# Two frequency pairs per filtered sum and half copy, under a newly written order of all instructions

## The chip, the cores and the metric

One core of one Trainium2 chip runs the whole kernel. The core's engines are TensorE (PE; its weight loads, PEld, overlap its matmuls), VectorE (DVE), ScalarE (ACT), GpSimd (POOL) and SyncE (SP), which here only issues DMAs. Each runs its own list of instructions in order and waits on semaphores for the others. The metric is the device time of one execution in microseconds (us). The kernel before takes 202.03 us (median of 3 runs, 201.94 to 202.16).

## The reference, cut to what matters

```python
x = A_x                                   # 1 x 2048 x 640, bf16
xn = layernorm(x)                         # over the 640 columns
X = rfft2(xn); X = X * (w_r + 1j * w_i)   # 2048 x 321 complex filter
A = irfft2(X, s=(2048, 640)).astype(bf16)
B = ((xn @ w_gate) * (xn @ w_up)) @ w_down   # 640 -> 1536 -> 640
return x + A + B
```

## The kernel before

The kernel computes the gated product (GLU) and the filtered spectrum in one program, so that TensorE always has matmuls of the one to run while the other engines prepare the other.

**Stages.** (1) Layer norm of 16 blocks of 128 rows (`bn`/`sm`/`sq`, `sd`, `rs`, `mul`), and transposes of the result. (2) GLU: each task `GU` is five matmuls of 512 columns (L951; the first blocks are smaller, L971), `eG` copies its PSUM bank to SBUF, and `H` multiplies gate and up (L987). (3) Column transform: `S1` to `S5` on DVE fold the 640 columns, `R` multiplies (L911), `eR` evicts. (4) The spectrum stage, described below. (5) Inverse over the columns: `I` (L1145), `eI`, `V1` to `V5` on DVE, `IV` (L1234). (6) `ACC` accumulates the GLU's second product (L1222) in a PSUM bank in three chunks (5, 4 and 3 matmuls, the last number of its name being 0, 5 or 9), `IV` adds the inverse transform into the same bank, `FINA` evicts it, `FIN` adds x, and a DMA stores it.

**The spectrum stage** runs over 16 steps t, each with two frequency pairs q = 2t and 2t+1:

- `D_t_0`, `D_t_1` (five matmuls each, L1028), evicted by `eD` (two copies of 64x321 each);
- `C_t` (two matmuls of 321 columns, L1048), which needs both `eD` of the step;
- `WM_t` on DVE: four products of 128x256 with the filter (L1065) into buffer PR, and two of 128x130 (L1071) into buffer Y5;
- `SM_t` on DVE: real and imaginary part of the filtered spectrum from PR, a subtraction on partitions 0 to 63 (L1080) and an addition on 64 to 127 (L1081), each 64x512, into buffer L;
- `JA_t` and `JB_t`: copies of the two halves of L across the partitions, the second negated, each 64x512, each on ACT or on DVE as the order says;
- `NS_t` on POOL: three copies inside Y5;
- `IA_2t`, `IA_2t+1` (four matmuls on L, L1114, two on Y5, L1116), evicted by `eIA` (128x320) into Z2. All 16 `I` need the whole of Z2, so all 32 `eIA`.

PR has two buffers of one step, L and Y5 three (`yr = t % 3`), the SBUF copy of D three.

**What sets the order.** `_PLAN` is one list of triples: task number, engine (0 PE, 1 ACT, 2 DVE, 3 POOL, 4 SP) and first PSUM bank (or -1). `replay` turns it into each engine's own list and derives the waits from reads, writes and bank owners. Nothing is decided at run time: an engine whose next instruction waits stands still, whatever lies behind it. PSUM has 8 banks; a matmul task that takes a bank waits for the evictions of the bank's last owner.

Of the kernel before, what the change touches and what calls it, by code (L numbers as in the profile page):

```python
# [369 lines left out]
_NY = 3  # L370
# [29 lines left out]
def _d_act(n):  # L400
# [4 lines left out]
    (12, 4, -1), (0, 1, -1), (13, 4, -1), (176, 1, -1), (175, 4, -1), (8, 2, -1), (18, 2, -1), (19, 2, -1), (20, 2, -1),  # L405
    (9, 3, -1), (29, 2, -1), (21, 1, -1), (23, 2, -1), (22, 2, -1), (11, 0, 0), (24, 2, -1), (25, 0, 2), (28, 2, -1),
    (30, 2, -1), (33, 2, -1), (177, 4, -1), (10, 0, 4), (178, 4, -1), (27, 2, -1), (14, 4, -1), (15, 4, -1), (31, 1, -1),
    (26, 1, -1), (185, 0, 5), (32, 2, -1), (34, 2, -1), (35, 0, 6), (179, 4, -1), (187, 0, 4), (36, 1, -1), (37, 2, -1),
    (180, 4, -1), (181, 4, -1), (38, 2, -1), (186, 1, -1), (39, 2, -1), (188, 1, -1), (189, 2, -1), (40, 2, -1), (192, 0, 0),
    (48, 2, -1), (41, 1, -1), (182, 4, -1), (197, 0, 1), (190, 0, 2), (198, 1, -1), (43, 2, -1), (195, 0, 3), (193, 1, -1),  # L410
    (16, 4, -1), (202, 0, 6), (42, 2, -1), (183, 4, -1), (196, 1, -1), (184, 4, -1), (44, 2, -1), (47, 2, -1), (1, 4, -1),
    (49, 2, -1), (191, 1, -1), (45, 0, 7), (200, 0, 5), (194, 2, -1), (17, 4, -1), (52, 2, -1), (50, 1, -1), (51, 2, -1),
    (2, 4, -1), (46, 1, -1), (53, 2, -1), (199, 2, -1), (205, 0, 4), (118, 2, -1), (201, 1, -1), (203, 1, -1), (54, 0, 5),
    (204, 2, -1), (207, 0, 1), (55, 1, -1), (3, 4, -1), (206, 1, -1), (210, 0, 0), (208, 1, -1), (119, 2, -1), (209, 2, -1),
    (211, 1, -1), (217, 0, 3), (120, 2, -1), (68, 1, -1), (215, 0, 2), (59, 2, -1), (69, 1, -1), (212, 0, 7), (57, 2, -1),
    (56, 2, -1), (60, 2, -1), (58, 2, -1), (4, 4, -1), (121, 2, -1), (218, 1, -1), (61, 2, -1), (220, 0, 6), (222, 0, 3),
    (213, 1, -1), (216, 1, -1), (214, 2, -1), (5, 4, -1), (62, 1, -1), (6, 4, -1), (122, 2, -1), (63, 2, -1), (70, 1, -1),
    (225, 0, 7), (219, 2, -1), (125, 0, 4), (71, 1, -1), (221, 1, -1), (7, 4, -1), (226, 1, -1), (230, 0, 2), (72, 1, -1),
    (64, 2, -1), (227, 0, 1), (66, 2, -1), (127, 2, -1), (123, 0, 6), (223, 1, -1), (73, 2, -1), (224, 2, -1), (128, 2, -1),
    (65, 4, -1), (78, 1, -1), (67, 4, -1), (231, 1, -1), (232, 0, 0), (76, 2, -1), (237, 0, 3), (129, 2, -1), (79, 1, -1),  # L420
    (228, 1, -1), (74, 2, -1), (80, 1, -1), (233, 1, -1), (235, 0, 2), (229, 2, -1), (81, 1, -1), (82, 1, -1), (236, 1, -1),
    (130, 2, -1), (75, 4, -1), (234, 2, -1), (83, 2, -1), (238, 1, -1), (240, 0, 1), (88, 1, -1), (242, 0, 0), (241, 1, -1),
    (131, 2, -1), (77, 4, -1), (84, 2, -1), (243, 1, -1), (85, 4, -1), (89, 1, -1), (126, 1, -1), (245, 0, 2), (247, 0, 3),
    (124, 1, -1), (134, 0, 0), (90, 1, -1), (246, 1, -1), (239, 2, -1), (86, 2, -1), (91, 1, -1), (92, 1, -1), (136, 2, -1),
    (244, 2, -1), (137, 2, -1), (87, 4, -1), (248, 1, -1), (252, 0, 4), (250, 0, 5), (93, 2, -1), (437, 4, -1), (132, 0, 6),
    (257, 0, 2), (249, 2, -1), (255, 0, 3), (438, 4, -1), (439, 4, -1), (251, 1, -1), (98, 1, -1), (138, 2, -1), (253, 1, -1),
    (260, 0, 5), (258, 1, -1), (254, 2, -1), (262, 0, 4), (139, 2, -1), (99, 1, -1), (256, 1, -1), (100, 1, -1), (440, 4, -1),
    (261, 1, -1), (441, 4, -1), (101, 1, -1), (263, 1, -1), (259, 2, -1), (267, 0, 2), (265, 0, 3), (272, 0, 5), (102, 1, -1),
    (96, 2, -1), (442, 4, -1), (266, 1, -1), (140, 2, -1), (270, 0, 4), (103, 2, -1), (443, 4, -1), (444, 4, -1), (268, 1, -1),
    (133, 1, -1), (264, 2, -1), (141, 0, 2), (94, 2, -1), (275, 0, 6), (104, 2, -1), (445, 4, -1), (108, 1, -1), (277, 0, 7),  # L430
    (142, 1, -1), (269, 2, -1), (446, 4, -1), (271, 1, -1), (145, 0, 2), (106, 2, -1), (273, 1, -1), (135, 1, -1), (280, 0, 4),
    (149, 2, -1), (276, 1, -1), (147, 0, 0), (278, 1, -1), (274, 2, -1), (150, 2, -1), (281, 1, -1), (447, 4, -1), (282, 0, 5),
    (279, 2, -1), (109, 1, -1), (146, 1, -1), (143, 0, 6), (285, 0, 4), (110, 1, -1), (448, 4, -1), (111, 1, -1), (477, 4, -1),
    (290, 0, 2), (287, 0, 3), (283, 1, -1), (151, 2, -1), (286, 1, -1), (291, 1, -1), (478, 4, -1), (288, 1, -1), (284, 2, -1),
    (152, 2, -1), (292, 0, 5), (112, 1, -1), (297, 0, 4), (479, 4, -1), (289, 2, -1), (148, 1, -1), (113, 2, -1), (153, 2, -1),
    (300, 0, 2), (293, 1, -1), (116, 2, -1), (144, 1, -1), (95, 4, -1), (97, 4, -1), (298, 1, -1), (114, 2, -1), (302, 0, 3),
    (294, 2, -1), (295, 0, 0), (307, 0, 1), (160, 0, 6), (156, 0, 4), (162, 2, -1), (105, 4, -1), (107, 4, -1), (301, 1, -1),
    (480, 4, -1), (296, 1, -1), (299, 2, -1), (303, 1, -1), (163, 2, -1), (158, 0, 2), (161, 1, -1), (305, 0, 0), (308, 1, -1),
    (154, 0, 6), (312, 0, 1), (481, 4, -1), (304, 2, -1), (159, 1, -1), (310, 0, 2), (482, 4, -1), (483, 4, -1), (317, 0, 3),
    (484, 4, -1), (306, 1, -1), (315, 0, 0), (155, 1, -1), (164, 2, -1), (318, 1, -1), (311, 1, -1), (115, 4, -1), (313, 1, -1),  # L440
    (157, 1, -1), (316, 1, -1), (309, 2, -1), (165, 2, -1), (322, 0, 6), (117, 4, -1), (320, 0, 7), (166, 2, -1), (319, 2, -1),
    (167, 0, 2), (323, 1, -1), (321, 1, -1), (314, 2, -1), (169, 0, 4), (168, 1, -1), (435, 4, -1), (170, 2, -1), (171, 0, 0),
    (173, 0, 6), (436, 4, -1), (172, 2, -1), (729, 4, -1), (513, 4, -1), (514, 4, -1), (324, 2, -1), (174, 1, -1), (325, 0, 2),
    (449, 0, 3), (515, 4, -1), (450, 2, -1), (326, 1, -1), (451, 0, 4), (465, 0, 5), (463, 0, 6), (452, 1, -1), (327, 0, 7),
    (453, 0, 0), (487, 0, 4), (485, 0, 2), (516, 4, -1), (464, 1, -1), (466, 2, -1), (454, 2, -1), (330, 0, 3), (501, 0, 5),
    (458, 3, -1), (335, 0, 6), (517, 4, -1), (328, 1, -1), (329, 2, -1), (467, 0, 0), (455, 2, -1), (486, 1, -1), (518, 4, -1),
    (468, 2, -1), (488, 1, -1), (519, 4, -1), (523, 0, 7), (331, 1, -1), (502, 1, -1), (337, 0, 2), (336, 1, -1), (332, 0, 3),
    (521, 0, 6), (499, 0, 4), (489, 0, 0), (456, 2, -1), (469, 2, -1), (340, 0, 5), (338, 1, -1), (520, 4, -1), (524, 1, -1),
    (342, 0, 2), (549, 4, -1), (457, 2, -1), (535, 0, 7), (333, 1, -1), (472, 3, -1), (461, 0, 3), (334, 2, -1), (522, 1, -1),
    (500, 1, -1), (459, 0, 6), (471, 1, -1), (490, 2, -1), (343, 1, -1), (550, 4, -1), (339, 2, -1), (345, 0, 4), (460, 1, -1),  # L450
    (503, 0, 0), (470, 1, -1), (352, 0, 2), (557, 0, 6), (491, 2, -1), (341, 1, -1), (551, 4, -1), (462, 1, -1), (504, 2, -1),
    (552, 4, -1), (536, 1, -1), (473, 0, 5), (347, 0, 3), (344, 2, -1), (559, 0, 7), (537, 0, 0), (475, 0, 1), (553, 4, -1),
    (505, 2, -1), (474, 1, -1), (353, 1, -1), (492, 2, -1), (508, 3, -1), (346, 1, -1), (506, 2, -1), (350, 0, 2), (494, 3, -1),
    (525, 0, 4), (476, 1, -1), (554, 4, -1), (555, 4, -1), (556, 4, -1), (348, 1, -1), (493, 2, -1), (349, 2, -1), (507, 2, -1),
    (355, 0, 1), (526, 2, -1), (360, 0, 3), (558, 1, -1), (495, 0, 6), (351, 1, -1), (354, 2, -1), (511, 0, 2), (538, 1, -1),
    (356, 1, -1), (497, 0, 0), (571, 0, 1), (361, 1, -1), (539, 0, 4), (585, 4, -1), (496, 1, -1), (586, 4, -1), (527, 2, -1),
    (587, 4, -1), (540, 2, -1), (357, 0, 3), (498, 1, -1), (362, 0, 6), (572, 1, -1), (595, 0, 0), (509, 0, 1), (358, 1, -1),
    (560, 1, -1), (365, 0, 3), (588, 4, -1), (596, 1, -1), (529, 2, -1), (573, 0, 7), (589, 4, -1), (512, 1, -1), (359, 2, -1),
# [67 lines left out]
def _build(nc, A_x, A_w_r, A_w_i, B_w_gate, B_w_up, B_w_down, out, opts=None):  # L526
# [3 lines left out]
    with es:  # L530
# [32 lines left out]
        b_g = alloc("G", 640)  # L563
        b_sm = alloc("SM", 384)
        b_gbf = alloc("GBF", 6 * 512)
        b_stat = alloc("STAT", 768)
        b_dum = alloc("DUM", 256)
        b_jk = alloc("JK", 640)

# [776 lines left out]
```

## Time and profile before

| | |
|---|---|
| median of 3 runs | 202.03 us |
| profiled execution: own time, span | 201.94 us, 200.1 us |
| busy: PE, DVE, ACT, POOL | 194.3, 179.1, 141.7, 24.8 us |
| granted TensorE clock | 1.000 |
| SM: 32 instructions of 64x512 on DVE | 422 and 420 ns each |
| JA on DVE, JA on ACT (64x512) | 12 of 298 ns, 4 of 628 ns |
| JB on DVE, JB on ACT (64x512) | 9 of 289 ns, 7 of 628 ns |

The profile's busy times say how long an engine had at least one instruction in flight; neighbouring instructions on one engine overlap a little, so an engine that never waits follows its own list at a spacing somewhat under the duration of an instruction. Matmul ends are modelled, so the spacing from one start to the next says more on PE than the busy time. The span runs from the first to the last instruction; 1.8 us of the execution lie around it.

### The profile page before, as it was taken

To read this page: it belongs to the slowest core of one execution; us is meant where nothing else is said; L and a number is where in the kernel's file an instruction comes from. 1 tells how busy PE (TensorE), PEld (TensorE's weight loads), DVE (VectorE), ACT (ScalarE), POOL (GpSimd) and SP (SyncE) were. 2 spreads that over 40 slices of the span, in tenths; PEclk is the share of its full clock that TensorE was granted. 3 is DMA by queue.
4 is the path that set the end of the run, shared out by engine and by line. 5 is a ranking of instruction groups with operands and counts; after the bars stand their busy time and mean duration, and the time that the engine had idled before them with its cause. 6 is when DMAs were issued, how large, how long until landed. Compare 5 with 4: busy or idle time off the path is not lost.

```text
span 200.1 us, 4335 instructions
## 1 busy us (share of the span) xinstructions
PE 194.3 (97%) x1623; PEld 123.3 (62%) x1623; DVE 179.1 (89%) x418; ACT 141.7 (71%) x309; POOL 24.8 (12%) x53
## 2 busy tenths in 40 slices
PE   7799999999999999999999999999999999999995
PEld 7698644445455555555555554547777777777774
DVE  3799999999999999989999989978999999899803
ACT  3377999999965989999999999996504541442311
POOL 0000000000000006056335333630000000000000
DMA  6999985428438351351452420006101325033422
GB/s 182 307 332 385 375 132 123 114 58 98 103 65 268 110 133 38 97 128 38 113 150 54 118 64 6 0 3 183 50 0 63 86 84 164 33 101 112 142 80 66
DMA packets 29669, 23.80 MB, mean 119 GB/s; under 512 B 10576, under 2 KB 27600, under 8 KB 29520
## 3 DMA queue, kind: packets, MB, share of 16 engines
q1 hardware_dynamic: 28848, 23.16, 42.1%
q10 hardware_dynamic: 800, 0.36, 0.7%
q8 instruction: 13, 0.21, 0.5%
q14 instruction: 8, 0.07, 0.1%
HBM read 18.92 MB, written 2.62 MB: 108 GB/s over the span
## 4 chain that ended last, share of the span: by engine, by line
PE 53%; ACT 26%; DVE 15%; issue 4%; DMA 1%
PE ps L1222 26%; ACT arena L687 20%; PE ps L951 12%; PE ps L971 6%; DVE arena L987 2%; PE ps L1145 2%; PE ps L1234 2%; ACT arena L750 2%; ACT arena L741 2%; ACT arena L1091 2%; DVE arena L863 1%; PE ps L1028 1%; DMA arena<-in_A_x_dram 1%; DVE arena L864 1%; PE ps L1048 1%
## 5 line engine op out<-in xcount | busy, mean ns | idle before, releaser
L687 ACT ACTIVATE arena<-ps 128x512 bf16<-128x512 f32 (+7 forms) x247 | 118.2, 529 | 47.2 <-PE ps L1234 21.1
L951 PE MATMUL ps<-arena 128*128 128x512 bf16 x420 | 98.1, 379 | 0.7 <-ACT arena L687 0.4
L951 PEld LDWEIGHTS ps<-arena 128*128 128x128 bf16 x420 | 38.4, 98 | 42.6 <-ACT arena L687 3.2
L1222 PE MATMUL ps<-arena 128*128 128x320 bf16 (+2 forms) x396 | 57.3, 295 | 0.0
L1222 PEld LDWEIGHTS ps<-arena 128*128 128x128 bf16 x396 | 37.6, 98 | 13.2
L1065 DVE TENSOR_TENSOR arena<-ps,arena 128x256 bf16<-128x256 f32 x64 | 22.7, 416 | 0.8 <-PE ps L1048 0.4
L1100 POOL COPY arena<-arena 128x126 bf16<-128x126 bf16 x16 | 6.6, 414 | 108.7 <-DVE arena L1071 108.7
L987 DVE TENSOR_TENSOR arena<-arena 128x512 bf16<-128x512 bf16 x42 | 17.4, 417 | 1.7 <-ACT arena L687 1.3
L971 PE MATMUL ps<-arena 128*128 128x128 bf16 (+1 forms) x160 | 14.1, 246 | 0.8 <-DVE arena L785 0.8
L971 PEld LDWEIGHTS ps<-arena 128*128 128x128 bf16 x160 | 12.3, 98 | 1.9 <-DMA arena<-in_B_w_gate_dram 0.8
L1261 DVE TENSOR_TENSOR arena<-arena 128x640 bf16<-128x640 bf16 x15 | 7.2, 486 | 6.1 <-ACT arena L687 6.1
L1102 POOL TENSOR_SCALAR arena<-arena 128x130 bf16<-128x130 bf16 x16 | 11.4, 715 | 0.0
L1028 PEld LDWEIGHTS ps<-arena 128*128 128x128 bf16 x160 | 7.5, 98 | 4.1 <-issue 0.4
L1114 PEld LDWEIGHTS ps<-arena 128*128 128x128 bf16 x128 | 7.6, 120 | 3.7 <-ACT arena L687 1.5
L1114 PE MATMUL ps<-arena 128*128 128x64 bf16 x128 | 8.9, 200 | 0.4 <-ACT arena L687 0.3
L688 DVE CAST arena<-ps 64x321 bf16<-64x321 f32 (+3 forms) x14 | 7.7, 577 | 1.6 <-PE ps L1116 1.1
L1028 PE MATMUL ps<-arena 128*128 128x64 bf16 (+1 forms) x160 | 8.5, 193 | 0.0
L750 ACT ACTIVATE arena<-arena 128x640 bf16<-128x640 bf16 x10 | 8.4, 839 | 0.1
L1071 DVE TENSOR_TENSOR arena<-ps,arena 128x130 bf16<-128x130 f32 x32 | 8.0, 293 | 0.0
L759 DVE BATCH_NORM_STATS2 arena<-arena 128x6 f32<-128x320 bf16 x12 | 5.3, 477 | 2.9 <-DMA arena<-in_A_x_dram 2.8
L863 DVE TENSOR_TENSOR arena<-arena 128x768 f32<-128x768 bf16 (+1 forms) x10 | 7.9, 789 | 0.0
L1101 POOL COPY arena<-arena 128x126 bf16<-128x126 bf16 x16 | 7.8, 490 | 0.0
(66 smaller groups left out, 211.9 us busy)
## 6 DMA issues: line engine op xcount, KB each, us to landing
arena<-in_A_x_dram SPq DMA_DIRECT2D x20, 160.0 KB, 2.6
arena<-in_A_w_r_dram SPq DMA_DIRECT2D x30, 80.2 KB, 2.2
arena<-in_A_w_i_dram SPq DMA_DIRECT2D x30, 80.2 KB, 2.2
out_dram<-arena SPq DMA_DIRECT2D x15, 160.0 KB, 1.8
arena<-in_B_w_gate_dram SPq DMA_DIRECT2D x4, 320.0 KB, 5.4
arena<-in_A_x_dram SPq DMA_DIRECT2D x1, 1280.0 KB, 10.0
arena<-c_tf SPq DMA_DIRECT2D x4, 256.0 KB, 10.2
arena<-c_ti SPq DMA_DIRECT2D x2, 512.0 KB, 5.3
```

Source lines behind the costliest of these rows:

```text
L687: return c.e.activation(dst, src, _ACTF.Copy)
L750: return c.e.activation(v_jk, v_x[:, b, :], _ACTF.Square, scale=-1.0, bias=v_m32[:, b:b + 1], accum_out=v_ss[:, b:b + 1])
L863: c.e.tensor_tensor(uo[:, o, :, 0:3, :], v_xb[:, b:b + nt, 0:6:2, :], v_xb[:, b:b + nt, 5:10:2, :], op)
L951: ins = c.e.matmul(ps[:, bk, :], v_gw[:, w, j, ft, :], v_xt[:, j, rows], start=(j == 0), stop=(j == 4))
L971: ins = c.e.matmul(ps[:, bk, w * n:(w + 1) * n], v_gw[:, w, j, ft, :], v_xt[:, j, rows], start=(j == 0), stop=(j == 4))
L987: return c.e.tensor_tensor(v_ht[:, ft0, rows], v_gbf[:, rr, 0, :], v_gbf[:, rr, 1, :], _OP.mult)
L1028: ins = c.e.matmul(ps[:, bk, k * 64:k * 64 + n], v_uq[:, k, t, :], v_fd[:, k * 128 + w * n: k * 128 + w * n + n], start=True, stop=True)
L1065: c.e.tensor_tensor(dst, xh, wv, _OP.mult)
L1071: ins = c.e.tensor_tensor(d5[w], ps[:, bk:bk + 2, 256:321], wt[:, w, :, 0:321:5], _OP.mult)
L1102: return c.e.tensor_scalar(yg[:, :, 128:193], yg[:, :, 256:321], -1.0, None, _OP.mult)
L1114: c.e.matmul(ps[:, bk, 64 * k:64 * k + 64], yl[:, k:512:4], v_ti[:, q, 0, :], start=True, stop=True)
L1222: ins = c.e.matmul(ps[:, bk, 0:sl3.stop - sl3.start], v_ht[:, ft, a * 128:(a + 1) * 128], v_wd[:, ft, sl3], start=(ft == _FT_ORDER[0]), st ...
```

## The change

1. `SM`, `JA` and `JB` run once for two steps: the loop leaves at even t after `NS_t`; at odd t one `SM_t` takes both steps' products (64x1024 per instruction), one `JA_t` and one `JB_t` copy 64x1024, and the four `IA` (and `eIA`) of the two steps follow. 48 tasks (64 instructions) become 24 (32 instructions).
2. Buffers: PR becomes one buffer of two steps, L two buffers of two steps (4096 elements instead of 3072). Y5 keeps three buffers of one step. STAT is 160 elements shorter, so what is allocated behind it moves by that much.
3. `_PLAN` is new throughout: order on every engine, engine of each eviction and half copy, PSUM banks. The list of SP is the same, entry by entry; POOL's differs in the order of a few `NS`.

```diff
-        b_pr = alloc("PR", 2 * 1024)
-        b_l = alloc("L", _NY * 1024)
+        b_pr = alloc("PR", 2048)
+        b_l = alloc("L", 2 * 2048)
...
-                        dst = v_pr[:, pb, w].rearrange("p g (h m k) -> p h g m k", h=2, k=4)[:, h]
+                        dst = v_pr[:, w, 2 * pb:2 * pb + 2].rearrange("p g (h m k) -> p h g m k", h=2, k=4)[:, h]
...
-            def em_sm(c, pb=pb, yr=yr):
-                pa_, pb_ = v_pr[:, pb, 0], v_pr[:, pb, 1]
-                c.e.tensor_tensor(v_l[0:64, yr, :, 0, :], pa_[0:64], pb_[64:128], _OP.subtract)
-                return c.e.tensor_tensor(v_l[64:128, yr, :, 0, :], pa_[64:128], pb_[0:64], _OP.add)
-            T("SM_%d" % t, "dve", 886.0, em_sm, reads=[(b_pr, ("r", pb, pb + 1))],
-              writes=[(b_l, ("r", 3 * yr, 3 * yr + 1))], prio=pq - 0.001)
...
+            if t % 2 == 0:
+                continue
+            lr = (t // 2) % 2
+
+            def em_sm(c, lr=lr):
+                pa_, pb_ = v_pr[:, 0], v_pr[:, 1]
+                c.e.tensor_tensor(v_l[0:64, lr, :, 0, :], pa_[0:64], pb_[64:128], _OP.subtract)
+                return c.e.tensor_tensor(v_l[64:128, lr, :, 0, :], pa_[64:128], pb_[0:64], _OP.add)
+            T("SM_%d" % t, "dve", 1420.0, em_sm, reads=[(b_pr, ("r", 0, 2))],
+              writes=[(b_l, ("r", 3 * lr, 3 * lr + 1))], prio=pq - 0.001)
...
+            for q in range(2 * t - 2, 2 * t + 2):
+                g, tq = q % 2, q // 2
+                yr = tq % _NY
```

The engine lists that the two plans give, counted by task:

| | ACT before | ACT after | DVE before | DVE after |
|---|---|---|---|---|
| SM | | | 16 | 8 (double) |
| JA | 4 | 3 (double) | 12 | 5 (double) |
| JB | 7 | 0 | 9 | 8 (double) |
| eD (two copies each) | 29 | 30 | 3 | 2 |
| eG | 97 | 95 | 3 | 5 |
| eR | 14 | 15 | 2 | 1 |
| eIA | 29 | 27 | 3 | 5 |
| eI | 15 | 14 | 1 | 2 |

All other counts are equal. Three stretches of the new lists, by name, that the prediction follows:

```
PE  (into the spectrum stage): 56 GU tasks in all, then R_15 R_12 R_13 GU_2_8_0 R_14 GU_2_8_1 D_0_1 D_1_0 D_0_0 D_1_1
    (before:                   56 GU tasks in all, then R_12 R_13 R_14 R_15 GU_2_8_0 D_0_0 D_0_1 D_1_1 D_1_0)
PE  (end of it): C_14 GU_9_12_0 IA_24 IA_25 C_15 GU_11_12_1 GU_11_12_0 IA_27 ACC_1_1_0 IA_26 GU_10_12_0 ACC_0_0_0
    IA_28 IA_30 IA_31 IA_29 ACC_0_0_5 I_1 I_0 I_2 ACC_1_1_5 I_3 I_6 ACC_0_1_0 ACC_2_0_0 I_4 ACC_0_1_5 ACC_2_0_5 ACC_0_1_9 I_7
    (before: C_15 GU_10_12_0 IA_27 GU_11_12_0 IA_26 IA_29 GU_10_12_1 IA_28 IA_30 IA_31 GU_11_12_1 I_3 ACC_1_0_0 I_2 I_0 I_1)
DVE (same stretch): H_46 JB_13 JA_13 WM_14 WM_15 SM_15 JA_15 JB_15 eIA_28 eIA_31 eG_49_1 eI_0 H_47 V1_0 V2_0 V3_0 V4_0 V5_0
```

## The prediction

> **What bounds the kernel now.** I read the page's busy times first, then the same by stretch, then who waited for whom, then the chain that ended last.
>
> ```profile
> PE 194.3 (97%) x1623; PEld 123.3 (62%) x1623; DVE 179.1 (89%) x418; ACT 141.7 (71%) x309; POOL 24.8 (12%) x53
> ```
>
> By stretch (its length, then PE, PEld, DVE, ACT and POOL busy, clock, DMA):
>
> ```profile
> 14.00:68.30 54.30, 54.19 (x331) 29.54 (x329) 54.27 (x116) 48.51 (x107) 0.00 (x0) 1.00 0.66 175
> 68.30:136.60 68.30, 67.11 (x624) 36.93 (x625) 62.90 (x183) 65.53 (x142) 24.51 (x48) 1.00 0.27 69
> 136.60:197.90 61.30, 61.24 (x511) 45.68 (x508) 52.35 (x90) 21.64 (x45) 0.00 (x0) 1.00 0.29 93
> ```
>
> Three regimes: 14 to 68.3 PE and DVE are both full; in the spectrum stage (68.3 to 136.6) ACT is 96% busy, DVE 92%; behind it PE alone is full. The busy PE of the middle row overstates PE, because a matmul's record covers the one before it. Its spacing tells more:
>
> ```profile
> 78.80 2.16 PE ps L951 x10
> 97.11 1.72 ACT arena L687 x4
> 107.59 0.44 ACT arena L687
> 137.79 0.84 PE ps L1145 x15
> 143.96 6.79 PE ps L1222 x50
> ```
>
> These are chain lines (start, length, what). Without a wait a matmul of 512 columns follows the next after 0.216 us, of 320 after 0.136, of 128 after 0.056. The timeline gives 0.137 for 321 columns, 0.029 for 64, 0.035 in IA. In the spectrum stage that makes 220 x 0.216 + 160 x 0.029 + 128 x 0.035 + 64 x 0.029 + 32 x 0.137 + 20 x 0.056 = 64.0 us of work in 68.3: 4.3 us of PE are lost. Over the whole span the same sum is 190.5 us; about 6.2 us are lost between the first and last matmul: 1.8 before 13 us (first loads, first layer norm), 0.7 from 68.3 to 72.7, 3.7 from 80 to 134, none after. So the most that this change can win where it acts is 4.4 us. Who makes PE wait:
>
> ```profile
> PEld ps L951 <- ACT arena L687: 3.2, 14, 0.4
> PEld ps L1114 <- ACT arena L687: 1.5, 3, 0.7
> PEld ps L911 <- ACT arena L687: 0.6, 1, 0.6
> DVE arena L987 <- ACT arena L687: 1.3, 3, 0.7
> ```
>
> ACT, by its evictions (engine, line, waited for: total, times, longest), in many waits under half a microsecond. The chain of 97 to 131 us is ACT instruction behind ACT instruction. ACT's list is what the spectrum stage lasts.
>
> The Trainium skill (Perfetto Trace Analysis, Identifying the Most-Contended Engine) says that matmul busy time misjudges PE and that weight-load busy time should be used; at 62% it would leave PE 38% of room, make DVE (89%) the engine to relieve, and promise what DVE sheds (1.6 us below, so 200.4). The spacing shows a PE with 5% of room and an ACT that holds it, so the sum goes by the spacing.
>
> **What it costs and frees.**
>
> ```profile
> L1080 DVE TENSOR_TENSOR arena<-arena 64x512 bf16<-64x512 bf16 x16 | 6.8, 422 | 0.5
> L1081 DVE TENSOR_TENSOR arena<-arena 64x512 bf16<-64x512 bf16 x16 | 6.7, 420 | 0.2
> L688 DVE COPY arena<-arena 64x512 bf16<-64x512 bf16 x12 | 3.5, 298 | 0.3
> L1092 DVE TENSOR_SCALAR arena<-arena 64x512 bf16<-64x512 bf16 x9 | 2.6, 289 | 0.3
> L1091 ACT ACTIVATE arena<-arena 64x512 bf16<-64x512 bf16 x7 | 4.4, 628 | 0.2
> L988 DVE TENSOR_TENSOR arena<-arena 128x512 bf16<-128x512 bf16 x4 | 1.6, 406 | 0.0
> L988 DVE TENSOR_TENSOR arena<-arena 128x256 bf16<-128x256 bf16 x4 | 1.1, 270 | 0.0
> L874 DVE TENSOR_TENSOR arena<-arena 128x1024 f32<-128x1024 f32 x3 | 3.6, 1212 | 0.0
> ```
>
> (Group rows: count, busy us, mean ns of one, idle before.) *SM:* 16 x (422 + 420) ns = 13.5 us leave DVE. The new 64x1024 form is in no row: from 256 to 512 columns L988 grows by 0.53 ns a column, which makes 421 + 512 x 0.53 = 0.69 us; the float32 row of 1024 gives 1.21. I take 0.69, the same operation and type: 16 x 0.69 = 11.1. DVE gains 2.4 us; by the other end it loses 5.9.
>
> *JA, JB on DVE:* 12 x 298 + 9 x 289 = 6.2 us leave. A two-element reciprocal takes 156 ns, so some 0.14 us of a copy grow with size: double ones take 0.44 and 0.42 (ends: 0.29 for no growth, 0.60 for two single ones): 5 x 0.44 + 8 x 0.42 = 5.6. *On ACT:* 11 x 628 = 6.9 leave; three double ones at 1.08 (ACT grows 0.89 ns a column from the 377 ns of 256 columns to the 604 of 512; ends 0.63 and 1.26): 3.2. *Moved evictions* by their rows: eD to ACT (DVE -0.98, ACT +0.87), eR to ACT (-0.82, +0.73), two eG to DVE (+1.36, -1.21), two eIA to DVE (+0.97, -0.88), one eI to DVE (+0.83, -0.70).
>
> Sums: DVE -13.5 + 11.1 - 6.2 + 5.6 + 1.4 = -1.6 us; ACT -6.9 + 3.2 - 1.2 = -4.9 us, nearly all in the spectrum stage, where ACT stood idle for 2.8 us of 68.3 and its work falls from 65.5 to about 61. PE's matmuls are unchanged; SP issues the same DMAs in the same order; NS on POOL gets up to a step more time.
>
> **What that is worth on PE.** I laid the three lists beside each other from R on, each at its own spacing (eG 0.49, eD 0.91, eIA 0.33 on ACT; WM 1.86, H 0.34 on DVE), with no waits, and compared. Before, an eviction eD comes between 3.5 us ahead and 0.4 us behind the C that needs it (C_10: 0.1 ahead, C_15: 0.4 behind), the last half copy of IA_29 is 0.9 behind. In the new lists the closest eD is 1.1 ahead (C_3), most are 3 to 8, the closest half copy 1.4 ahead (IA_7). So ACT no longer sets the stage; short waits on one bank or one eviction remain, also since JA_1 on ACT must now stand until the double SM_1, with eD_3_0 behind it (I find ACT about 1 us idle there, C_3 just met). I leave 1.0 of the 3.7 us: **-2.7**.
>
> *Entry (68.3 to 72.7).* The first R wait for S5_4. DVE's list up to S5_4 has the same 25 H and S tasks, 54.9 us without idle, so this wait (0.3) stays; R_14 now stands two GU ahead of the D, which takes most of the other 0.4: **-0.3**.
>
> *Exit.* The last chain is C_15, WM_15, SM_15, JA, JB, IA_28: 0.4 + 1.9 + 1.4 + 0.9 = 4.6 us; PE has from C_15 to IA_28 three GU (3.2), two IA (0.4), ten ACC matmuls (1.4) and C itself (0.3): 5.3, enough. The first I then waits for eIA_29, covered only by ACC_0_0_5 (0.54): **+0.2**.
>
> *Closing stage.* PE has 13.4 us from the first I to the first IV (13.9 before, three ACC chunks having gone ahead of I), against a chain of 1.8 (four I) + 0.7 (eI) + 10.6 (V1 to V5) = 13.1. Margin 0.3, 0.4 before. I add nothing; without that cover the price is the lateness itself. *First 14 us:* mul0 comes some 0.2 us earlier (bn1_1 moves behind it), but GU_3_0 waits at 8.62 us for the third up-weight load either way: **-0.1** for one later wait.
>
> *Buffers.* PR loses its second buffer, but writer (WM) and reader (SM) both run on DVE, in order: nothing. The skill's same page (Optimization Strategy) reads repeating bubbles as a sign of too few buffers, which speaks against this. The waits above end with ACT evictions, so I do not follow it.
>
> Sum: -2.7 - 0.3 + 0.2 - 0.1 = -2.9. The profiled execution took 201.94 us (span 200.1 and 1.8 around it), 0.09 under the median. 202.03 - 2.9 = **199.1 us**. Its own range, 0 to 2.3 us of remaining waits in the stage, is 198.0 to 200.4.
>
> **Rivals.** *Half of it only.* IA now waits for two steps, so a late C delays four IA and the evictions of their banks: 0.25 us for each of eight pairs gives 2.0 us back: 201.1 (200.4 to 201.6). For it: WM_7, WM_9, WM_11 start with their C, so DVE stands between pairs. Against: the margins above.
>
> *Slower: the double SM runs like the float32 row.* DVE's list in the stage, 60.6 us by spacing against 66.0 of PE (ACC chunks included), becomes 16 x 0.52 = 8.3 us longer: 69; with its waits for C, 3 to 4 us go to the end: about 205. It decides from about 0.33 us more per instruction, 1.02 us. For it only that the form is new; against, that it is L1080's own pattern with more groups.
>
> *Slower by order.* In 14 to 68 us DVE has no idle time, so each wait put into its list lengthens S5_4 one for one. The nearest is H_15, whose eG_15_0 stands 1.6 us later in ACT's list and was 0.33 us ahead. It decides from 3 us, 204.
>
> *Nothing:* the waits of PE are for banks, not for ACT's load, and come back: 201.9. Against: ACT idles only 2.8 us of the stage.
>
> **How the numbers follow.** Forecast 0.62, half 0.20, nothing 0.05, slower 0.13 (0.06 for SM, 0.07 for order). A change within 0.2% (0.4 us) cannot be told from none. Faster 0.82, same 0.05, slower 0.13. The range takes the forecast and the half, 197.9 to 201.6.
>
> **What would show it.** Right: 16 DVE rows of 64x1024 near 0.69 us; ACT in the spectrum stage near 61 us busy; PEld's waits for ACT L687 down from 5.3 to under 2; the chain through that stage more PE than ACT; span near 197.2. Wrong: SM over 1 us, DVE idle before 68 us, PE waiting for V5 behind 150 us.

## The result, and the profile after

The changed kernel took a median of 199.44 us (199.32 to 200.22, 4 runs) beside 201.99 us of the kernel before (201.85 to 202.16, 4 runs): ratio 0.9882, 95% interval 0.9855 to 0.9908. In another set of runs it was 199.62 us, ratio 0.988 [0.9866, 0.9894]. The forecast was 199.1 us, 197.9 to 201.6. The profiled execution took 199.54 us with a span of 197.2.

The page of the kernel after, its busy times and the shares of the chain that ended last:

```profile
PE 192.8 (98%) x1623; PEld 123.5 (63%) x1623; DVE 177.8 (90%) x396; ACT 138.0 (70%) x299; POOL 28.4 (14%) x53
PE 72%; ACT 13%; DVE 5%; SPq 4%; DMA 4%; issue 1%
```

The chain was PE 53%, ACT 26%, DVE 15% before. The same by stretch (length, then PE, PEld, DVE, ACT, POOL busy, clock, DMA); the middle row is the spectrum stage:

```profile
14.00:68.00 54.00, 53.78 (x329) 29.36 (x327) 53.89 (x115) 49.01 (x106) 0.00 (x0) 1.00 0.65 176
68.00:133.70 65.70, 65.23 (x610) 36.53 (x608) 61.04 (x160) 59.95 (x132) 28.15 (x48) 1.00 0.28 72
133.70:195.00 61.30, 61.20 (x528) 45.73 (x525) 53.04 (x91) 22.75 (x47) 0.00 (x0) 1.00 0.30 93
```

The first and the last stretch are within 0.3 us as long as they were; the middle one is 65.7 us in place of 68.3, ACT 91% busy in it and no longer 96%. POOL rose by 3.6 us, which no step of the prediction has. The waits on ACT's evictions (engine, line, waited for: total, times, longest), in the new line numbers:

```profile
PEld ps L948 <- ACT arena L684: 1.4, 4, 0.7
PEld ps L1025 <- ACT arena L684: 0.7, 2, 0.4
PEld ps L908 <- ACT arena L684: 0.4, 2, 0.2
```

From 5.3 us on three lines these came down to 2.5, and the view shows no `IA` that waits for ACT any more (L1114 before, 1.5 us). The double instructions, by groups:

```profile
L1089 DVE TENSOR_TENSOR arena<-arena 64x1024 bf16<-64x1024 bf16 x8 | 5.5, 688 | 0.3
L1090 DVE TENSOR_TENSOR arena<-arena 64x1024 bf16<-64x1024 bf16 x8 | 5.5, 686 | 0.1
L1101 DVE TENSOR_SCALAR arena<-arena 64x1024 bf16<-64x1024 bf16 x8 | 3.4, 422 | 0.3
L685 DVE COPY arena<-arena 64x1024 bf16<-64x1024 bf16 x5 | 2.1, 423 | 0.2
L684 ACT ACTIVATE arena<-arena 64x1024 bf16<-64x1024 bf16 x3 | 3.2, 1051 | 0.0
L1077 POOL COPY arena<-arena 128x126 bf16<-128x126 bf16 x16 | 9.3, 582 | 104.4 <-DVE arena L1068 104.4
```

The first five rows are the five prices of the forecast (0.69, 0.69, 0.42, 0.44, 1.08 us). The last, a POOL copy, was 414 ns.

Some pieces of the chain after (start, length, what):

```profile
92.96 2.16 PE ps L948 x10
95.54 2.16 PE ps L948 x10
128.65 0.45 ACT arena L684
129.14 2.33 PE ps L948 x10
135.66 1.00 PE ps L1147 x15
```

Where the chain before went from one ACT instruction to the next between 97 and 131 us, ten `GU` matmuls now follow ten others at 0.216 us each; the longest piece of ACT among them is the eviction at 128.65.

**PE's lost time.** Start-to-start distance less the undisturbed spacing gives what each stretch lost:

| | before | after | change | forecast |
|---|---|---|---|---|
| first 14 us: start of the `GU` that needs the third up-weight load (us) | 8.75 | 8.67 | -0.1 | -0.1 |
| entry: `R`, `D` at 68 to 73; after, one `GU` at 40.2 waits 0.39 for `H_13` | 0.72 | 0.39 | -0.3 | -0.3 |
| spectrum stage, 80 to 134 | 3.72 | 1.20 | -2.5 | -2.7 |
| exit: `I_1` waits for `eIA_29` | 0 | 0.19 | +0.2 | +0.2 |
| closing stage | 0 | 0 | 0 | 0 |
| end of the last matmul | 197.84 | 194.93 | -2.9 | -2.9 |

Some 0.2 us of the last row lies in no single wait. The time fell by 2.4 (profiled executions) to 2.55 us (medians), less than the span's 2.9, since what lies around the span was 1.8 us before and 2.3 after. What that half microsecond is, the trace does not show.

### The profile page after: what moved, and what is told of

The parts are those of the page before. It is cut to its first block, busy times and chain, and to the rows that moved or that the text cites. A ratio compares the mean times of both kernels' runs of the same rounds, so it can differ in the third digit from the quotient of the medians.

```text
span 197.2 us, 4300 instructions
## 1 busy us (share of the span) xinstructions
PE 192.8 (98%) x1623; PEld 123.5 (63%) x1623; DVE 177.8 (90%) x396; ACT 138.0 (70%) x299; POOL 28.4 (14%) x53
## 4 chain that ended last, share of the span: by engine, by line
PE 72%; ACT 13%; DVE 5%; SPq 4%; DMA 4%; issue 1%
PE ps L948 33%; PE ps L1224 26%; ACT arena L684 7%; SPq L678 4%; DMA arena<-in_A_x_dram 4%; ACT arena L747 3%; ACT arena L738 3%; PE ps L1147 2%; PE ps L1236 2%; PE ps L1116 2%; PE ps L1025 2%; PE ps L1045 2%; PE ps L908 2%; DVE arena L1062 1%; DVE arena L685 1%; PE ps L1118 1%
## 5 line engine op out<-in xcount | busy, mean ns | idle before, releaser
L684 ACT ACTIVATE arena<-ps 128x512 bf16<-128x512 f32 (+6 forms) x245 | 118.5, 525 | 49.5 <-PE ps L1236 21.1
L1224 PE MATMUL ps<-arena 128*128 128x320 bf16 (+2 forms) x396 | 57.2, 295 | 0.0
L1077 POOL COPY arena<-arena 128x126 bf16<-128x126 bf16 x16 | 9.3, 582 | 104.4 <-DVE arena L1068 104.4
L1079 POOL TENSOR_SCALAR arena<-arena 128x130 bf16<-128x130 bf16 x16 | 11.7, 728 | 0.0
L685 DVE CAST arena<-ps 128x512 bf16<-128x512 f32 (+3 forms) x15 | 8.4, 578 | 2.4 <-PE ps L1118 1.7
L1078 POOL COPY arena<-arena 128x126 bf16<-128x126 bf16 x16 | 8.6, 538 | 0.0
L1116 PE MATMUL ps<-arena 128*128 128x64 bf16 x128 | 8.4, 199 | 0.1
L1236 PE MATMUL ps<-arena 128*128 128x320 bf16 (+2 forms) x33 | 7.6, 295 | 0.0
```

The lines of the kernel that those rows point to most:

```text
L684: return c.e.activation(dst, src, _ACTF.Copy)
L685: return c.e.tensor_copy(dst, src)
L1079: return c.e.tensor_scalar(yg[:, :, 128:193], yg[:, :, 256:321], -1.0, None, _OP.mult)
L1116: c.e.matmul(ps[:, bk, 64 * k:64 * k + 64], yl[:, k:512:4], v_ti[:, q, 0, :], start=True, stop=True)
L1224: ins = c.e.matmul(ps[:, bk, 0:sl3.stop - sl3.start], v_ht[:, ft, a * 128:(a + 1) * 128], v_wd[:, ft, sl3], start=(ft == _FT_ORDER[0]), st ...
L1236: return c.e.matmul(ps[:, bank_of(own), 0:sl3.stop - sl3.start], v_sm[:, 2, :], v_v[:, a, sl3], start=False, stop=True)
```

## Experiments

Two theories at first. *ACT:* its list set the spectrum stage, and PE wins what ACT is relieved of. *Merge, or order alone:* what pays is the merged instructions (DVE's 1.3 us), or the new sequence whatever the engines carry.

**Order without the merge.** The kernel before under the new `_PLAN`, `SM`, `JA`, `JB` once per step.

```diff
-_PLAN = (order of before)
+_PLAN = (order of after; each SM_t, JA_t, JB_t preceded by SM_t-1, JA_t-1, JB_t-1 on the same engine)
```

> The new order with SM, JA and JB done once per step, as before the change (each double task is replaced by its two single ones, side by side, on the same engine). Theory ACT-and-merge: the new order has taken eight half copies off ACT, and it is the merging that lets DVE take them; without it DVE's list in the spectrum stage grows by 8 x (1.77 - 1.40) + 13 x (0.64 - 0.44) = 5.6 us, from 60.6 to 66.2, as long as PE's 66.0, and DVE becomes what the stage lasts: 201.0 to 203.0 us. Rival order-alone: the new order and its banks do it and the merging is along for the ride: 199.2 to 200.2 us.

Measured: 199.94 us (199.57 to 200.36), ratio 0.9891 [0.987, 0.9912]. Its stage, by the window:

```profile
68.00:134.30 66.30, 65.81 (x611) 37.11 (x609) 63.54 (x186) 61.00 (x135) 22.93 (x48) 1.00 0.29 71
```

Order alone brings 2.1 of the 2.5 us; the other 0.3 to 0.5 us, which would be the merge's, lie inside the intervals. The theory that DVE needs the merge to take the copies (201 to 203 us) is out. ACT is at 61.0 us here too: the order moved the half copies off ACT, merged or not.

**Merge without the order.** The kernel after, under the old list; `SM`, `JA`, `JB` stand at the odd step's place, and the `IA` of even steps are put behind them.

```diff
-_PLAN = (order of after)
+_PLAN = (order of before without SM, JA, JB of even t; what depends on them follows their odd partner)
```

> The double SM, JA and JB under the old order: tasks keep the old sequence, engines and banks, and only those that would come ahead of what they need are put back (mainly IA of even steps, behind the double half copies). ACT keeps five double half copies (5.4 us against 6.9 before, so 1.5 us less), DVE sheds some 4 us. Theory ACT-and-merge: only 1.5 of 4.9 us leave ACT, and the IA that were put back hold their banks' evictions up: 200.8 to 202.5 us. Rival merge-alone (the merging is worth it in any order): 199.2 to 200.2 us.

Measured: 214.95 us (214.77 to 216.21), ratio 1.0656 [1.0625, 1.0687]. Both theories missed by 12 us and more. A wait of this run, a piece of its chain, and the window around it:

```profile
DVE arena L1062 <- PE ps L1045: 17.1, 10, 5.0
```
```profile
122.96 0.29 PE ps L1045 x2
123.27 1.42 DVE arena L1062 x4
124.69 0.42 DVE arena L1068 x2
125.13 0.69 DVE arena L1089
125.83 0.70 DVE arena L1090
126.53 0.14 issue
126.66 0.70 PE ps L1045 x2
```
```profile
120.00:130.00 10.00, 6.57 (x45) 3.25 (x44) 6.56 (x18) 5.63 (x13) 2.74 (x4) 0.83 0.12 34
```

`C`, `WM`, the double `SM` and the next `C` run one behind the other, and PE stands for 3.6 us with everything behind that `C` in its list. That `C` waits for the double `SM` because it also takes over, ahead of its `WM`, the buffer PR, of which there is now one, and the `SM` before must have read it; `WM` in turn waits 17.1 us for `C`. PE has seven waits over 1 us, 12.4 us together, five of them at an `IA` and two at a `C`. No engine is full in the window (PE 66%, DVE 66%, ACT 56%). A merge makes the first of two steps wait for the second; an order that was written without it puts PE in front of that wait again and again.

**ACT's half copies cut short.** The kernel before in its own order; copies on ACT take 16 columns a row, and the rest is left out.

```diff
-                return copy_on(c, v_l[0:64, yr, :, 1, :], v_l[64:128, yr, :, 0, :])
+                n = 16 if c.e is nc.scalar else 256
+                return copy_on(c, v_l[0:64, yr, :, 1, 0:n], v_l[64:128, yr, :, 0, 0:n])
```

(`JB` on ACT the same.)

> The kernel before with its 11 half copies on ACT cut from 256 to 16 columns of each pair (the other columns of the copies are left out, so the output is not the reference's); order, engines and banks are the old ones. ACT sheds 11 x 0.43 = 4.7 us in the spectrum stage, DVE nothing. Theory ACT: the 3.7 us that PE loses between 80 and 134 us fall to 0.8 to 1.7: 199.0 to 200.2 us. Rival DVE (the stage is paced by DVE's work, which the change lightens by 1.6 us): no change, 201.8 to 202.2. Rival banks (the waits are for banks and come back): 201.5 to 202.0.

Measured: 199.30 us (199.23 to 199.72), ratio 0.9863 [0.9842, 0.9884]. The chain of this run, and its wait of `GU` for ACT:

```profile
PE 94%; DVE 2%; DMA 1%; ACT 1%; issue 0%
```
```profile
PEld ps L951 <- ACT arena L687: 1.3, 6, 0.3
```

With ACT 4.3 us shorter and nothing else touched, the old order has all of the gain. A rival is that the copies themselves end sooner, and not that ACT has less to do. In the kernel before, each of PE's eight waits over 0.2 us between 97 and 134 us ends with an ACT eviction of the bank that PE takes next, and none with a half copy; `GU`'s wait for ACT came down from 3.2 to 1.3 us. So it is ACT's load that counts here. It also answers the rival "nothing" of the prediction: the waits are for banks, but ACT's list is what frees these.

**DVE shortened by as much.** The kernel before with `SM` as two copies, the sums left out.

```diff
-                c.e.tensor_tensor(v_l[0:64, yr, :, 0, :], pa_[0:64], pb_[64:128], _OP.subtract)
-                return c.e.tensor_tensor(v_l[64:128, yr, :, 0, :], pa_[64:128], pb_[0:64], _OP.add)
+                c.e.tensor_copy(v_l[0:64, yr, :, 0, :], pa_[0:64])
+                return c.e.tensor_copy(v_l[64:128, yr, :, 0, :], pa_[64:128])
```

> The kernel before with SM's 32 sums on DVE made plain copies of the first product (the subtraction and addition are left out, so the output is not the reference's); order, engines and banks are the old ones. DVE sheds 32 x 0.13 = 4.2 us in the spectrum stage (copy rows 0.29 us against 0.42), ACT nothing. Theory ACT: DVE runs ahead and waits, PE still loses 3 us or more: 201.4 to 202.1 us. Rival DVE: 199.2 to 200.5.

Measured: 202.08 us (201.91 to 202.58), ratio 0.9999 [0.9986, 1.0011]: nothing. The end of its stage, by the window, with the kernel before in the first row and this run in the second:

```profile
120.00:136.00 16.00, 15.41 (x144) 8.34 (x143) 14.00 (x42) 15.60 (x35) 6.29 (x12) 1.00 0.01 4
120.00:136.00 16.00, 15.41 (x144) 8.35 (x143) 12.97 (x42) 15.61 (x35) 5.18 (x12) 1.00 0.01 3
```

DVE fell from 14.00 to 12.97 us there, ACT stayed at 98% (15.60 before), and PE's time is the same to the hundredth. The Trainium skill (Perfetto Trace Analysis, Identifying the Most-Contended Engine) says that the engine with the highest occupancy is to be relieved first, and that PE is judged by MFU (its share of the peak rate) and by weight-load busy time. The prediction used the second alone, 62%, which left DVE at 89% of the span, ahead of ACT at 71%. By MFU PE itself comes first: its matmuls move 440,512 columns, and at the 0.216 us that 512 of them take without a wait this makes 186 of 200.1 us, an estimate of 93%. So these two runs speak against weight loads alone and against choosing between DVE and ACT over the whole span, and not against MFU: 4.2 us less on DVE gave nothing, 4.3 us less on ACT gave 2.7.

**The half copies moved, the order kept.** The kernel before with eight of ACT's eleven copies on DVE.

```diff
-JB_6 JB_9 JB_10 JB_12 JA_12 JB_13 JA_14 JB_14: engine 1 (ACT)
+JB_6 JB_9 JB_10 JB_12 JA_12 JB_13 JA_14 JB_14: engine 2 (DVE), at the same places of _PLAN
```

> The kernel before with eight entries of its order altered and nothing else: eight of the eleven half copies that ACT makes (JB of steps 6, 9, 10, 12, 13, 14 and JA of 12 and 14) go to DVE at the same place of the order. ACT sheds 8 x 0.65 = 5.2 us in the spectrum stage, DVE takes 8 x 0.32 = 2.6 us and stands at 65.2 of the 66 us that a stage without waits would last. Theory ACT's list (what counts is only that ACT is shorter, as when its copies were cut short): 199.3 to 200.5 us. Rival order (the engine flips need the new sequence round them, or DVE becomes the late one): 201.0 to 203.0.

Measured: 203.55 us (203.15 to 204.52), ratio 1.0081 [1.0058, 1.0104]: slower by 1.5 us, more than either theory had. A wait of this run in the stage (in weight loads), and its end by the window:

```profile
PEld ps L1114 <- issue: 2.6, 1, 2.6
```
```profile
120.00:136.00 16.00, 13.10 (x119) 7.18 (x120) 15.39 (x48) 11.52 (x27) 6.06 (x13) 1.00 0.04 11
```

ACT is relieved as meant (11.52 in place of 15.60), but PE's `IA_27`, of step 13, waits 2.28 us up to 133.8: the `JB_13` that it needs runs at 133.43 to 133.72, behind `WM_15` (131.59 to 133.40) in DVE's list. (The expectation of the next run names `JB_14` and `JA_14` for this wait; by the trace it is `JB_13`, which that run moves too.) "ACT is relieved, so PE gains" is not enough.

**The same copies right behind their SM.** So that no copy stands behind a later `WM`:

```diff
-... SM_14 H_46 WM_15 JB_13 JA_14 SM_15 JB_14 JB_15     (DVE, as above)
+... SM_13 JB_13 WM_14 H_45 SM_14 JA_14 JB_14 H_46 WM_15 SM_15 JB_15
```

> The kernel before, with the same eight half copies moved from ACT to DVE as in e9_j_to_dve (JB_6, 9, 10, 12, 13, 14, JA_12, 14), but each now stands directly behind its SM in DVE's list, and not where it stood in the common order. If e9 lost its time because a copy stood behind the next WM (JB_14 and JA_14 behind WM_15, 2.3 us of wait of PE at 133.8), and ACT's list is what the stage lasts: PE's waits of 2.28 and 0.82 us go, ACT stays near 61 us busy in the stage, 199.5 to 200.8 us. If work on DVE in this order is what costs (DVE's list is as long as in e9 and the WM now come later by 0.3 us a copy), the waits only move, and it stays at 202.5 to 204 us.

Measured: 202.15 us (201.94 to 203.53), ratio 1.0011 [0.9994, 1.0028]: the 1.4 us are back, and nothing is won. Its chain, then two windows:

```profile
DVE 48%; PE 33%; ACT 8%; issue 5%; DMA 3%; SPq 1%
```
```profile
100.00:120.00 20.00, 19.98 (x185) 10.98 (x183) 19.23 (x58) 18.54 (x43) 7.56 (x15) 1.00 0.37 97
120.00:136.00 16.00, 14.49 (x141) 8.28 (x141) 15.41 (x48) 11.84 (x27) 6.50 (x12) 1.00 0.01 2
```

PE's waits fell from 1.4 to 0.8 us between 97 and 120 us, and rose from 1.6 to 2.3 behind it, where five of the eight copies lie: DVE is 96% busy there, ACT 74%, and the waits left there are for `WM` and `H`, which the copies ahead of them in DVE's list push back: `C_14` waits 0.81 us for `WM_13`, `IA_26` 0.57 for `WM_15`, `C_13` 0.51 for `WM_12`, a `GU` 0.27 for `H_46`. The bound went from ACT to DVE within the stage.

**Both relieved.** The last one with `SM` as plain copies (the edit of the DVE run above).

> e10_j_placed with SM also cut to plain copies as in e4_dve_short (leaves out the sums; DVE some 4 us less). Each of the two edits alone left the time where it was (202.1). If the eight copies paid nothing because DVE was full where they landed (120 to 136 us: DVE 96% busy, ACT 74%), then with DVE relieved PE's waits of 0.81, 0.57 and 0.51 us behind 120 go and the whole gain appears: 199.2 to 200.4 us. If the old order itself holds the stage (C, IA and their evictions in the wrong sequence whatever the lists last), little changes: 201.4 to 202.2 us.

Measured: 199.96 us (199.81 to 200.07), ratio 0.989 [0.9865, 0.9914]. That closes a square on the old order:

| | DVE as it is | DVE 4 us shorter |
|---|---|---|
| ACT as it is | 202.0 | 202.1 |
| eight copies moved from ACT to DVE | 202.15 | 199.96 |

Neither edit alone gives anything, both give 2.0 us. ACT binds, and DVE stands so close behind that whoever moves ACT's work there must also find it room.

**Copies put back on ACT.** The kernel after with all eight double `JB` on ACT.

```diff
-JB_1 JB_3 ... JB_15: engine 2 (DVE)
+JB_1 JB_3 ... JB_15: engine 1 (ACT)
```

> The changed kernel with its eight double JB moved from DVE to ACT, at the same place of the order. ACT takes 8 x 1.05 = 8.4 us more in the spectrum stage (60.0 us busy of 65.7 in the trace), DVE sheds 3.4. Theory ACT's list: 68 us of ACT do not fit into 65.7, and IA wait for the copies besides: 202 to 205 us, slower than before the change, with PE waiting for ACT. Rival merge (the double sums and copies give the gain, whoever makes them): 199.2 to 200.5.

Measured: 210.98 us (209.59 to 211.17), ratio 1.0441: the direction is ACT's, at over twice the price. A window and two waits of the run:

```profile
80.00:90.00 10.00, 8.29 (x79) 4.45 (x79) 7.86 (x24) 9.78 (x21) 4.09 (x7) 1.00 0.39 100
```
```profile
ACT arena L1100 <- DVE arena L1090: 2.8, 3, 2.0
PEld ps L1116 <- ACT arena L1100: 1.9, 1, 1.9
```

ACT is 98% full, and besides its load it stands still for `SM` (2.8 us), with the evictions behind it. The expectation (202 to 205 us) had counted ACT's 8.4 us and `IA`'s waits for the copies, not ACT's own waits for `SM`. Some 1.4 us of the median goes with the clock: four of its five executions had a mean granted clock of 0.992 and took 210.98 to 211.17 us, the profiled one had 1.00 and took 209.59.

**More work for DVE.** The kernel after with one more 64x896 instruction per pair, into a scratch tile.

```diff
+                c.e.tensor_tensor(d_, pa_[0:64, :, 0:224], pb_[64:128, :, 0:224], _OP.subtract)
                 c.e.tensor_tensor(v_l[0:64, lr, :, 0, :], pa_[0:64], pb_[64:128], _OP.subtract)
```

> The kernel after, with one more 64x896 TENSOR_TENSOR per pair of steps, written to a scratch tile ahead of SM: about 0.62 us x 8 = 5.0 us more on DVE, 0.31 us for each of the 16 SM instructions, just short of the point (0.33) at which the prediction's rival on a slow SM was to decide. By the prediction's lists (DVE 4.7 us short of PE in the stage) most of it is hidden: 199.7 to 201.2 us. If DVE has no such slack where it matters, because a C, WM, SM, J, IA chain is late by what each SM is late, PE waits 0.4 to 0.6 us at each of eight pairs: 203 to 205 us.

Measured: 201.31 us (200.97 to 202.49), ratio 0.9959 [0.9947, 0.9971] to the kernel before, so 1.7 to 1.9 us over the kernel after, just above the first range. Its row of the new instruction, and the end of the stage:

```profile
L1091 DVE TENSOR_TENSOR arena<-arena 64x896 bf16<-64x896 bf16 x8 | 5.0, 621 | 0.3
```
```profile
120.00:136.00 16.00, 15.58 (x136) 8.35 (x133) 15.51 (x41) 13.18 (x30) 8.46 (x13) 1.00 0.08 22
```

Of 5.0 us, 3.2 are hidden and 1.8 come through; DVE is at 97% at the end of the stage. The slack that the lists promised is there, but not where each pair needs it. `C_2`, `C_4` and `C_14` wait 0.44, 0.30 and 0.27 us for the `SM` of the pair before, which must have read the one buffer PR.

**Single waits mended.** The waits left in the kernel after are mostly one instruction in line behind another. First `NS_12` ahead of `NS_13` (and 6 ahead of 7) on POOL, beside the kernel after again; then two more neighbours.

```diff
-POOL: NS_13 NS_12     NS_7 NS_6
+POOL: NS_12 NS_13     NS_6 NS_7
```

> The changed kernel, unaltered, beside the next three on one chip, so that they can be told apart from it at half a per cent. Expected 199.2 to 199.7 us.

> The changed kernel with NS_12 ahead of NS_13 and NS_6 ahead of NS_7 on POOL, nothing else. In the changed kernel's trace IA_24 waited 0.29 us for NS_12, which stood behind NS_13, and GU_11_12_1 then 0.22 us for the eviction of IA_24. Theory (those two waits are the order of POOL): span 0.2 to 0.4 us shorter, 199.0 to 199.3 us. Rival (C_15's eviction eD_15_0, 0.2 us behind, takes their place): no change.

```diff
+DVE: H_13 mul11           (was mul11 H_13)
+ACT: JA_1 eD_3_0 eG_31_1  (was JA_1 eG_31_1 eD_3_0)
```

> The kernel after with four neighbours exchanged, one for each wait of PE that its trace shows and that comes from the order alone: H_13 ahead of mul11 on DVE (0.39 us at 40.2), eD_3_0 ahead of eG_31_1 on ACT (0.45 us at 82.3), NS_12 ahead of NS_13 (0.29 us at 128.3) and NS_6 ahead of NS_7 on POOL. If each wait counts for itself, as the prediction's sum has it, 1.0 to 1.2 us less than the kernel after: 198.4 to 198.9 us. If the next instruction in line is late anyway, 0.2 to 0.5 us less: 199.1 to 199.5 us.

Measured: 199.62 (199.46 to 199.96) for the kernel after, 199.45 (199.28 to 199.58) with `NS` exchanged, 199.43 (199.35 to 199.72) with all four, a ratio of 0.9863 [0.985, 0.9875]. None is distinguishable from the kernel after. With `NS` exchanged the 0.29 us wait of `IA_24` goes, and the time does not show it. In the last, `D` no longer waits 0.45 us at 82.3, but the `IA` next to it waits 0.8 us, for the eviction `eG_31_1` that now stands behind `eD_3_0` on ACT (waits of that run):

```profile
PEld ps L1116 <- ACT arena L684: 0.8, 1, 0.8
PEld ps L948 <- ACT arena L684: 0.7, 2, 0.4
```

The stage is balanced to a few tenths, and a wait that is taken away shows up at the next instruction.

## Why the prediction was right, step by step

- *What binds.* ACT's list in the stage: shown by shortening it (-2.7 us) and by shortening DVE's (0).
- *The double instructions.* `SM` 688 and 686 ns (0.69 forecast), `JB` 422 (0.42), `JA` 423 on DVE (0.44) and 1051 on ACT (1.08). Extending the bf16 rows by their growth per column held; the float32 row was no guide.
- *DVE -1.6, ACT -4.9.* Busy times fell by 1.3 and 3.7. The counts are as forecast. The durations of ACT's records, added up, fell by 5.9 us (160.6 to 154.7), beside 141.7 and 138.0 us of busy time: the records overlap by 18.9 us before and 16.7 after, so busy time shows less; those of DVE fell by 1.2 (203.7 to 202.6). The forecast of 4.9 for ACT lies between the two. In the stage ACT has 59.95 us (61 forecast); PEld's waits for ACT came to 2.5 us, not to under 2.
- *-2.7 in the stage.* -2.5. The 1.0 us left for short waits became 1.2, and the case named, `eD_3_0` behind `JA_1` with `C_3` "just met", was the largest: 0.45 us, of the `D_4_1` that takes the bank of `eD_3_0`, with `C_3` right behind it. The margins of the lists held in direction, not in size: the closest eviction was to be 1.1 us ahead of its `C`, and `C_7` and `C_15` start 0.2 us behind theirs; `IA_7` starts 0.5 us behind its last copy in place of 1.4. A 0.29 us wait of `IA_24` for `NS_12` was not foreseen: the prediction gave POOL "up to a step more time" and priced no slower POOL.
- *-0.3 at the entry.* The sum holds, the place does not: the waits at 68 to 73 go completely, and a new one of 0.39 us stands at 40.2, where `mul11` was put ahead of `H_13` on DVE. The prediction looked for such a wait at `H_15`, where none appeared. DVE's list up to `S5_4` still ends at 68.2 us in both traces, so the time that PE stands at 40.2 is time that `R` need not wait later. That end, which the prediction took as fixed, sets the sum.
- *Exit +0.2, closing stage 0, start -0.1.* As forecast; no PE wait behind 136 us, though the closing margin was put at only 0.3.
- *The 0.3 us too little in the time* (199.1 against 199.44) is not in the span, which is 197.2 as named, but around it (2.3 us in place of 1.8).
- *Buffers, nothing.* The price is right, the reason is not the whole one. `WM` and `SM` do run in order on DVE, but in the kernel it is `C`, on PE, that takes over what its `WM` writes, so with one PR buffer the `C` of an even step waits for the `SM` of the pair before. In the kernel before the `SM` that `C` needed ended 2.1 to 4.4 us ahead of it; after, it ends 0.34 to 1.59 us ahead (0.34 at `C_2`, 0.51 at `C_4`). No wait over 0.15 us comes of it in the kernel after, but the merge under the old order has `C_12` wait 3.6 us and `C_2` 1.0 us for it. The term is nothing by the new order alone.
- *Rival "half of it".* "IA now waits for two steps" cost nothing that can be measured in the new order, which is no faster without the merge. In the old order the merge cost 13 us: the mechanism is real, and its price is the order's.
- *Rival "SM slow".* "Decides from about 0.33 us more per instruction": at 0.31 more the kernel is still 0.4% ahead of the kernel before, with two thirds of the gain gone. So the point lies above 0.31; the size was of the right order, and where exactly it lies was not measured.
- *What the prediction had too simple:* it took ACT's relief as the cause and DVE's as "nothing new". On the old order the same relief bought by load on DVE gives nothing. Why the new order makes do without the merge's room (199.94 with DVE at 180.6 us busy and ACT 138.5, against 202.15 with 181.2 and 137.2) follows from where the work stands in the lists, since loads are nearly equal; which of its some hundred moves does it was not tried.

## What to carry to other kernels

Find the engine that binds in the stage, not over the span, and test it by shortening its instructions in place. Before moving its work, look at the busy share of the receiving engine in the same 15 us, and at what it will stand behind there: here 74% on one engine and 96% on the other were worth no more than 98% and 88%. When steps of a pipeline are merged, look at the order with it, and at who takes over the buffers: here the same merge was 13 us slower under the old order.

## What the runs showed of the hardware that was not expected

POOL's copies depend on what DVE does at the time. In the kernel after, those of L1077 take 288 ns when no DVE instruction between SBUF tiles lies beside them (2 of 16) and 624 in the mean when one does; L1078 takes 290 (6 of 16) and 688, L1079 542 (6 of 16) and 840. Beside a `WM`, which reads one input from PSUM, a copy keeps its 288 ns. Beside a double `SM` of 688 ns seven copies of L1077 took 807 to 809 ns, and beside a single one of 420 ns in the kernel before 514 to 519: the copy ends some 0.1 us behind the DVE instruction that it started beside. So the price follows the length of DVE's instruction, and merging raised it: `NS` of odd steps took 2.2 to 2.4 us and of even steps 1.0 to 1.5 (1.2 to 1.6 each before), and the late `NS_12` held `IA_24`. With `SM` as plain copies on the old order, POOL was busy for 21.3 us and not 24.8. The Trainium skill (Advanced Engine Details and Errata, GPSIMD Details) says that the pool engine shares a read and a write interface with DVE and conflicts with DVE instructions that run in a two-port mode or read two SBUF inputs. These runs agree for instructions with two SBUF inputs, and add the price; whether the half copies run in a two-port mode no run shows.

After PE had stood for 3.6 us (the merge under the old order, up to 126.7 us), the clock record is 0.50 for 3.4 us from 126.3 us on, which makes 0.83 of the window shown, so a long wait cost more than itself. No other kept trace had a PE wait over 2.3 us in the stage, and none showed a clock under 1.00 there. Executions without a trace did have a lower mean clock: 0.991 and 0.992 in two of six with the half copies moved (204.5 us, the others 203.15 to 203.57), and 0.992 in four of five with all `JB` on ACT. So a run with PE waits near 2.3 us can have it or not; how long PE must stand, no run shows.
